# Relu-squared attention into a token mixer on one core: another opening, and key turns of 64 rows in two DMAs

## The chip, the cores and the metric

The kernel runs on one core of a Trainium2 chip. A core has four compute engines, each with an instruction queue of its own that is worked off in order: TensorE (PE; its weight loads are listed as PEld), VectorE (DVE), ScalarE (ACT) and GpSimd (POOL). SyncE (SP) issues DMAs, which 16 DMA engines carry out. TensorE writes to PSUM, from where DVE and ACT copy to SBUF. The metric is the time of one execution on the device in microseconds (us).

## The reference

There are 8 batches of 3200 tokens. With u and v of width 256 and z of width 64, the first half computes

```
scores = (z @ z.T) / S
attn   = max(scores, 0) ** 2
x      = u * (attn @ v)
```

and the second half mixes the tokens of x with three weight matrices:

```
q = x @ w_q ;  k = x @ w_k            # width 64
mixed = (q @ k.T / 8) @ x             # no softmax
out = max(mixed, 0) @ w_out
```

Since nothing nonlinear stands between q, k and x, the kernel computes the small matrix H = k.T @ x (64 x 256) per batch and then q @ H.

## The kernel before, in words

The 3200 rows of a batch are 25 tiles of 128. The columns of the score matrix are cut into seven groups: six of 512 and one of 128 (`widths`). For each group the kernel makes score tiles of 128 x 512, two at a time (a pair, `scores`), in a PSUM tile of two banks; two such tiles ("slots") exist, and all that is not an accumulator goes through them. A pair passes two stages: `first_stage` takes max(x, 0) times 4 on ACT or DVE (tile `g`), `second_stage` squares it on ACT, POOL or rarely DVE (tile `at`, `NAT` buffers). Products of `at` with v accumulate in four other banks (`acc00` to `acc11`, two halves of a group, and two row halves of TensorE, which work at the same time). The attention matrix is symmetric, so part of the `at` tiles are turned by DMA (`tt`) and serve as weights of another group.

When a half of a group is accumulated, ACT or DVE copies one bank, DVE adds the other (`both`), POOL multiplies by u (`x_sb`), and a DMA on SP turns x (`xT_sb`). Then `projections` gives q and k of the group stacked over 128 partitions (`qk`): for r = 0 the queries lie in the upper 64 rows and the keys in the lower, for r = 1 the other way round. `turn_keys` turns the keys by DMA, `heads` multiplies them with x, `heads_out` adds the result to `hacc`, and after a batch's last group the sum `hss` is formed. `mix`, `mix_out`, `proj`, `proj_out` make the output of a batch during the next batch; the last batch's output is made at the end, in a tail written out by hand.

Before the change the turn takes all 128 rows of `qk`, queries too, and `double_keys` on POOL then overwrites the turned queries with a copy of the keys, so that a 128-column weight holds the keys twice and both halves of `hacc` hold the same sums.

The order of all instructions is written by a planner in the kernel: a clock per engine (`clock`), `give(engine, ready, weight)` that books work, `move` and `flush` for DMAs on SP with due times, `at_time` for things at a planned time, `add_extra` for projections, mixes and output products. Constants steer it: `BIAS`, `LATE`, `XWAIT`, `UNTIL`, `lead` (how many score pairs are made ahead), `KEEP`. Before `UNTIL` a pair may be split in two halves on two engines. The planner's costs set the order alone; the chip runs that order by semaphores.

The opening is written by hand. z of batch 0 comes in four pieces (`ZCH`: tiles 0-3, 12-17, 18-24, 4-11), is cast and laid out twice (`cast_first`) and turned on TensorE (`turn_first`); v comes in four pieces on POOL's queue (`load_first_v`). Products on the identity (`warm`) fill TensorE until the first turn.

## Time and profile before

| | |
|---|---|
| median of three runs | 778.13 us (776.56 to 780.9) |
| the profiled execution | 776.21 us, its span 774.4 us |
| busy in the span | PE 99%, ACT 71%, POOL 78%, DVE 67% |
| TensorE busy from 20 to 740 us | 718.54 of 720.00 us |
| TensorE busy from 740 us to the end | 28.61 us |
| DMA queue of SP | 82.6% of 16 engines' span |

A line of a group or timeline gives the source line, engine, operation and tiles (written <- read), the shapes, the count, the duration, and in brackets the idle time of that engine before it and what ended it.

### The profile page before, as it was taken

To read this page: it belongs to the slowest core of one execution; us is meant where nothing else is said; L and a number is where in the kernel's file an instruction comes from. 1 tells how busy PE (TensorE), PEld (TensorE's weight loads), DVE (VectorE), ACT (ScalarE), POOL (GpSimd) and SP (SyncE) were. 2 spreads that over 40 slices of the span, in tenths; PEclk is the share of its full clock that TensorE was granted. 3 is DMA by queue.
4 is the path that set the end of the run, shared out by engine and by line. 5 is a ranking of instruction groups with operands and counts; after the bars stand their busy time and mean duration, and the time that the engine had idled before them with its cause. 6 is when DMAs were issued, how large, how long until landed. Compare 5 with 4: busy or idle time off the path is not lost.

```text
span 774.4 us, 28287 instructions
## 1 busy us (share of the span) xinstructions
PE 762.9 (99%) x12410; PEld 673.8 (87%) x12410; DVE 518.8 (67%) x550; ACT 548.5 (71%) x635; POOL 603.2 (78%) x510
## 2 busy tenths in 40 slices
PE   7999999999999999999999999999999999999996
PEld 6889999889898888988889888998889988898884
DVE  6687687766676566766667657675676756765545
ACT  6686777577666677776877767787587777677734
POOL 7789688888787679867879878778866778878941
PEclk9999999999999999999999999999999999999999
DMA  7999999999999979999999988999999998889745
GB/s 184 157 167 184 133 191 164 169 196 200 187 219 186 198 200 189 174 188 185 207 186 185 201 199 149 198 171 174 229 195 189 161 237 168 162 176 206 144 91 190
DMA packets 307115, 141.10 MB, mean 182 GB/s; under 512 B 285744, under 2 KB 288432, under 8 KB 306992
## 3 DMA queue, kind: packets, MB, share of 16 engines
q1 hardware_dynamic: 300224, 123.13, 82.6%
q0 software_dynamic: 6624, 15.98, 14.8%
q8 instruction: 97, 1.59, 0.9%
q10 hardware_dynamic: 144, 0.20, 0.1%
q14 instruction: 26, 0.21, 0.1%
HBM read 59.64 MB, written 26.21 MB: 111 GB/s over the span
## 4 chain that ended last, share of the span: by engine, by line
PE 94%; DVE 2%; DMA 2%; POOL 1%; issue 0%; ACT 0%; POOLq 0%; DVEq 0%; SPq 0%
PE acc L353 69%; PE sc L265 13%; PE fo L520 6%; PE qk L419 3%; PE qk L457 2%; PE mx L485 1%; DMA v_sb<-in_v_dram 1%; DVE g L291 1%; POOL x_sb L390 1%; DMA z<-in_z_dram 0%; DVE fo L542 0%; DMA xT_sb<-x_sb 0%; DVE both L371 0%; POOL at L310 0%; DVE both L370 0%
## 5 line engine op out<-in xcount | busy, mean ns | idle before, releaser
L353 PE MATMUL acc<-v_sb,at 64*128 64x256 f16 x7344 | 500.8, 269 | 1.3 <-POOL at L310 0.8
L310 POOL TENSOR_TENSOR at<-g 128x1024 f16<-128x1024 f32 (+2 forms) x232 | 414.4, 1799 | 84.8 <-DVE g L291 46.3
L353 PEld LDWEIGHTS <-at 64*128 64x128 f16 x7344 | 403.1, 94 | 52.8 <-issue 7.2
L291 DVE TENSOR_SCALAR g<-sc 128x1024 f32<-128x1024 f32 (+1 forms) x294 | 341.2, 1181 | 107.5 <-PE sc L265 97.4
L307 ACT ACTIVATE at<-g 128x1024 f16<-128x1024 f32 (+1 forms) x250 | 251.3, 1021 | 27.3 <-DVE g L291 24.1
L287 ACT ACTIVATE g<-sc 128x1024 f32<-128x1024 f32 (+2 forms) x184 | 180.5, 984 | 76.6 <-PE sc L265 72.0
L265 PE MATMUL sc<-zT 64*128 64x512 f16 x924 | 186.5, 375 | 2.4 <-DVE g L291 1.4
L390 POOL TENSOR_TENSOR x_sb<-both,u_sb 128x512 f16<-128x512 f32 (+1 forms) x112 | 135.6, 1215 | 63.7 <-DVE both L371 62.9
L353 PE MATMUL acc<-v_sb,tt 64*128 64x256 f16 x2272 | 162.7, 269 | 0.0
L353 PEld LDWEIGHTS <-tt 64*128 64x128 f16 x2272 | 126.6, 94 | 11.1
L371 DVE TENSOR_TENSOR both<-acc,both 128x512 f32<-128x512 f32 (+1 forms) x104 | 69.7, 671 | 23.6 <-ACT both L370 18.7
L265 PEld LDWEIGHTS <-zT 64*128 64x128 f16 x924 | 61.9, 94 | 7.9 <-issue 4.0
L370 ACT COPY both<-acc 128x512 f32<-128x512 f32 (+1 forms) x63 | 36.0, 571 | 45.7 <-PE acc L353 41.8
L542 DVE TENSOR_SCALAR fo<-fo 128x1024 f32<-128x1024 f32 (+2 forms) x30 | 33.1, 1116 | 42.7 <-PE fo L520 42.6
L508 ACT ACTIVATE rt<-mx 128x1024 f16<-128x1024 f32 (+1 forms) x46 | 42.5, 926 | 12.8 <-PE mx L485 12.7
L520 PE MATMUL fo<-wo,rt 128*128 128x256 f16 x400 | 49.5, 274 | 0.1
L370 DVE COPY both<-acc 128x512 f32<-128x512 f32 (+1 forms) x41 | 27.3, 665 | 31.3 <-PE acc L353 28.5
L520 PEld LDWEIGHTS <-rt 128*128 128x128 f16 x400 | 36.4, 98 | 10.7 <-issue 6.5
L433 ACT CAST qk<-qk 128x512 f16<-128x512 f32 (+1 forms) x45 | 24.4, 542 | 25.3 <-PE qk L457 22.7
L547 ACT ACTIVATE fo<-fo 128x1024 f32<-128x1024 f32 (+2 forms) x28 | 24.4, 871 | 23.7 <-PE fo L520 23.0
L472 DVE TENSOR_TENSOR ha<-qk,ha 128x512 f32<-128x512 f32 x37 | 25.5, 688 | 16.7 <-ACT qk L433 16.2
L419 PE MATMUL qk<-xT_sb,wqk 64*128 64x256 f16 (+1 forms) x404 | 32.8, 266 | 0.0
(47 smaller groups left out, 276.4 us busy)
## 6 DMA issues: line engine op xcount, KB each, us to landing
u_sb<-in_u_dram SPq DMA_DIRECT2D x48, 512.0 KB, 4.7
out_dram<-fo SPq DMA_DIRECT2D x46, 512.0 KB, 4.2
v_sb<-in_v_dram POOLq DMA_DIRECT2D x35, 320.0 KB, 6.1
zn<-in_z_dram POOLq DMA_DIRECT2D x7, 400.0 KB, 5.9
tt<-at SPq DMA_TRANSPOSE x143, 4.5
u_sb<-in_u_dram SPq DMA_DIRECT2D x8, 128.0 KB, 3.0
out_dram<-fo SPq DMA_DIRECT2D x8, 128.0 KB, 3.5
out_dram<-fo SPq DMA_DIRECT2D x4, 256.0 KB, 2.6
```

Of the source, the lines that this page charges most:

```text
L265: nc.tensor.matmul(out=sc[:, h, 0:gw], lhsT=z_cols(b, h, ti * P, P), rhs=z_cols(b, h, gs, gw), start=True, stop=True,)
L287: nc.scalar.activation(out=g[:, hs, 0:w], in_=sc[:, hs, 0:w], func=RELU, scale=GSCALE)
L291: nc.vector.tensor_scalar(out=g[:, hs, 0:w], in0=sc[:, hs, 0:w], scalar1=0.0, scalar2=GSCALE, op0=AOP.max, op1=AOP.mult,)
L307: nc.scalar.square(out=out, in_=g[:, hs, 0:w])
L310: mul(out=out, in0=g[:, hs, 0:w], in1=g[:, hs, 0:w])
L353: nc.tensor.matmul(out=accs[half, r][:, ds((j % 2) * D, D)], lhsT=weights(b, gi, ti, j)[top(r), :], rhs=vs[b][top(r), ti, :], start=(first ...
L370: copy(out=both[:, 0 : n * D], in_=accs[half, 0][:, 0 : n * D])
L371: nc.vector.tensor_add(out=both[:, 0 : n * D], in0=accs[half, 1][:, 0 : n * D], in1=both[:, 0 : n * D])
L390: nc.gpsimd.tensor_mul(out=xs[b, gi][:, 0:n, :, r, :].rearrange("p n c d -> p (n c) d"), in0=both[:, 0 : n * D].rearrange("p (m d) -> p m ...
L419: nc.tensor.matmul(out=ps[:, r, 0 : n * P], lhsT=wqk[top(r), c, :, :].rearrange("p t h -> p (t h)"), rhs=xTs[b, gi][top(r), 0:n, c, :], st ...
L508: nc.scalar.activation(out=out, in_=part, func=RELU)
L520: nc.tensor.matmul(out=banks[r][:, ds(j * D, D)], lhsT=flat[:, ds((dc * n + j) * P, P)], rhs=wo[:, dc, :], start=(dc == 0 and j == 0), sto ...
```

## The change

- *Opening.* The warming products read a cleared piece of a weight tile (`blank`) instead of the identity, and are 36; the later five are gone. v's first piece is issued ahead of the identity, its second right after it, its last by the planner at 7.5 us. `first_pair` puts the first pair into two accumulator banks, so that ACT and DVE each take a half. Pairs are no longer split later in the first stage; `UNTIL` is 12 and `on_act` takes ACT at a tie.
- *Keys.* `turn_keys` turns only the 64 rows that hold keys, in one DMA for each r, into one of three tiles of five 64-column blocks. `heads` reads blocks n and n+1 as one 128-column weight: the first 64 output rows are the wanted sums, the others are not used. `double_keys` is gone; `heads_out` adds 64 rows; `hss` is made by two POOL adds, one for each row half.
- *Buffers and planning.* 18 `at` buffers for 16, `KEEP` 4 for 6, `lead` 160 for 140, other `BIAS`, `LATE`, `XWAIT`, `V1`.
- *Tail.* The last batch's `hsum` is made by DVE and POOL, a half each.

```diff
-    NAT = 16
+    NAT = 18
     NX = 7
...
     NEARBY = 8
-    KEEP = 6
+    KEEP = 4
...
         ready = clock[PE] + FROM_PE
-        on_act = max(clock[ACT], ready) < max(clock[DVE], ready)
+        on_act = max(clock[ACT], ready) <= max(clock[DVE], ready)
         copy = nc.scalar.copy if on_act else nc.vector.tensor_copy
...
         for _ in range(n):
-            nc.tensor.matmul(out=idle[:, 0:P], lhsT=ident[:], rhs=ident[:], start=True, stop=True)
+            nc.tensor.matmul(out=idle[:, 0:P], lhsT=blank, rhs=blank, start=True, stop=True)
         clock[PE] += 0.053 * cold() * n
...
-    def scores(p):
+    def scores(p, banks=None):
         assert len(ztimes) >= 4 * tiles[2 * p + 1][0] and p_chunk(p) in z_at, (p, clock, len(ztimes), z_at)
-        sc = ps_tile("sc")
+        sc = banks or ps_tile("sc")
         for h, (b, gi, ti) in enumerate(tiles[2 * p : 2 * p + 2]):
...
             nc.tensor.matmul(
-                out=sc[:, h, 0:gw],
+                out=sc[h][:, 0:gw] if banks else sc[:, h, 0:gw],
                 lhsT=z_cols(b, h, ti * P, P),
...
         for (hs, w), on_act in zip(parts, ways * 2):
+            part = sc[hs.start][:, 0:w] if isinstance(sc, list) else sc[:, hs, 0:w]
             if on_act:
                 nc.scalar.activation(
-                    out=g[:, hs, 0:w], in_=sc[:, hs, 0:w], func=RELU, scale=GSCALE
+                    out=g[:, hs, 0:w], in_=part, func=RELU, scale=GSCALE
                 )
...
                 nc.vector.tensor_scalar(
-                    out=g[:, hs, 0:w], in0=sc[:, hs, 0:w], scalar1=0.0,
+                    out=g[:, hs, 0:w], in0=part, scalar1=0.0,
                     scalar2=GSCALE, op0=AOP.max, op1=AOP.mult,
...
+    kts = [pk.tile([P, 5, dh], FP16, tag=f"kx{i}", name="kx", bufs=1) for i in range(3)]
+
+    def clear_keys():
+        for kt in kts:
+            nc.gpsimd.memset(kt[:], 0.0)
+        give(POOL, 0.0, 0.3)
+
     def turn_keys(b, gi):
-        nn = widths[gi] // P
-        ks[b, gi] = pk.tile([P, 4, 2, dh], FP16, tag="kx", name="kx")
-        nc.sync.dma_start_transpose(
-            out=ks[b, gi][:, 0:nn, :, :].rearrange("p n a h -> p n (a h)"),
-            in_=qks[b, gi][:].rearrange("p r s -> p (r s)")[:, 0 : nn * P],
-        )
-
-    doubled = set()
-
-    def double_keys(b, gi):
-        doubled.add((b, gi))
-        nn = widths[gi] // P
+        n = min(2, widths[gi] // P)
+        ks[b, gi] = kts[(b * NG + gi) % len(kts)]
         for r in halves(gi):
-            sl = slice(2 * r, min(2 * r + 2, nn))
-            nc.gpsimd.tensor_copy(out=ks[b, gi][:, sl, r, :], in_=ks[b, gi][:, sl, 1 - r, :])
+            nc.sync.dma_start_transpose(
+                out=ks[b, gi][:, 2 * r : 2 * r + n, :],
+                in_=qks[b, gi][top(1 - r), r, 0 : n * P],
+            )
...
         nn = widths[gi] // P
-        assert (b, gi) in doubled
+        assert (b, gi) in keys_at
         for n in range(nn):
...
                     out=ps[:, r, D : 2 * D],
-                    lhsT=ks[b, gi][top(r), n, :, :].rearrange("p a h -> p (a h)"),
+                    lhsT=ks[b, gi][top(r), n : n + 2, :].rearrange("p a h -> p (a h)"),
                     rhs=x_rows(b, gi, n)[top(r), :, :],
...
     def heads_out(b, gi, ps):
-        part = ps[:, 0:2, D : 2 * D]
+        part = ps[0:dh, 0:2, D : 2 * D]
         if gi == 0:
-            hacc[b] = psml.tile([P, 2, D], FP32, tag="ha", name="ha")
+            hacc[b] = psml.tile([dh, 2, D], FP32, tag="ha", name="ha", bufs=1)
             nc.vector.tensor_copy(out=hacc[b][:], in_=part)
...
         if gi == LASTG:
-            heads_done(b)
-
-    def heads_done(b):
-        hss[b] = psml.tile([P, D], FP16, tag="hs", name="hs")
-        ha = hacc.pop(b)
-        nc.gpsimd.tensor_add(out=hss[b][:], in0=ha[:, 0, :], in1=ha[:, 1, :])
+            hss[b] = psml.tile([P, D], FP16, tag="hs", name="hs")
+            ha = hacc.pop(b)
+            for r in range(2):
+                nc.gpsimd.tensor_add(out=hss[b][top(r), :], in0=ha[:, 0, :], in1=ha[:, 1, :])
...
+    C3 = 7.0
+    T3 = 10.0
+    V3 = 7.5
     moves = []
...
     def cold():
-        return 2.0 if clock[PE] < 8.4 else 1.0
+        return 2.0 if clock[PE] < 4.6 else 1.0
...
     SPLIT = 0.2
-    UNTIL = 24.0
+    UNTIL = 12.0
...
         return a + BIAS < d
+
+    def first_pair():
+        produced[0] += 1
+        sc = scores(0, [acc_tile(0, r, "sc")[:] for r in range(2)])
+        clock[PE] += 0.22
+        ready = clock[PE] + FROM_PE
+        a, d = give(ACT, ready, 0.6), give(DVE, ready, 0.69)
+        free_at[0] = max(a, d)
+        g = first_stage(0, sc, [True, False])
+        for x, t in zip(tiles, (give(ACT, a, 0.63), give(POOL, d, 1.05))):
+            row_at[x] = t + 0.3
+        for (b, gi, gj, _, nn, _, _), turn in second_stage(0, g, [True, False]):
+            raise AssertionError((b, gi, gj))
...
         a, d = (max(clock[x], ready) for x in (ACT, DVE))
-        if clock[PE] < UNTIL and max(a + 0.57, d + 0.68) + SPLIT < min(a + 1.03, d + 1.2):
-            ways = [a < d, a >= d]
-            done = max(give(ACT, ready, 0.57), give(DVE, ready, 0.68))
-        else:
-            ways = [choose(a, d)]
-            done = give(ACT, ready, 1.03) if ways[0] else give(DVE, ready, 1.2)
+        ways = [choose(a, d)]
+        done = give(ACT, ready, 1.03) if ways[0] else give(DVE, ready, 1.22)
         g = first_stage(p, sc, ways)
...
             ways = [2 if by_dve else by_act]
-            if clock[PE] < UNTIL and max(a + 0.57, c + 0.97) + SPLIT < min(a + 1.06, c + 1.9):
+            if clock[PE] < UNTIL and max(a + 0.63, c + 1.05) + SPLIT < min(a + 1.06, c + 1.9):
                 ways = [a < c, a >= c]
-                done = max(give(ACT, ready, 0.57), give(POOL, ready, 0.97))
+                done = max(give(ACT, ready, 0.63), give(POOL, ready, 1.05))
             else:
...
                 row_at[b, gj, starts[gi] // P + n] = t + 0.5
-
-    def double(b, gi):
-        keys_at[b, gi] = give(POOL, clock[PE], 0.6) + 0.5
-        double_keys(b, gi)
...
             move(
-                done + SLACK, done + 10.0, 1.28, 0.21 * n, lambda: turn_keys(b, gi),
-                lambda t: at_time(t, lambda: double(b, gi)),
+                done + SLACK, done + 10.0, 1.28 * len(halves(gi)), 0.105 * n, lambda: turn_keys(b, gi),
+                lambda t: keys_at.update({(b, gi): t + 0.3}),
             )
...
             if prior[1] == LASTG:
-                give(POOL, done, 0.6)
+                give(POOL, done, 1.4)
                 heads_known(prior[0])
...
         if prior[1] == LASTG:
-            give(POOL, done, 0.6)
+            give(POOL, done, 1.4)
             heads_known(prior[0])
...
     V0 = 56
-    V1 = 11
+    V1 = 8
...
             t0 = max(t + 6, Z0)
-            if b == 0:
-                nc.gpsimd.memset(zn[:, 0 : NT + 2 : NT + 1, :], 0.0)
             at_time(t0, lambda: (load_z(b + 1), push(3.0)))
...
     MORE = 3.0
-    BIAS = 0.2
+    BIAS = -0.2
     XDUE = 5.0
-    XWAIT = 2.0
-    LATE = 0.3
+    XWAIT = 7.0
+    LATE = 0.5
...
-    make_identity(nc, ident)
+    blank = wo[:, 0, 0:P]
+    nc.vector.memset(blank, 0.0)
+    nc.vector.memset(zn[:, 0 : NT + 2 : NT + 1, :], 0.0)
     load_first_z()
     load_first_v(0, 4)
-    idle = acc_tile(0, 1, "warm")
-    warm(28)
+    make_identity(nc, ident)
+    load_first_v(12, 6)
+    idle = acc_tile(1, 0, "warm")
+    warm(36)
     cast_first(0)
...
     cast_first(2)
-    load_first_v(12, 6)
     load_first_v(18, 7)
-    load_first_v(4, 8)
-    clock[:] = [4.4, 4.75, 4.3, 7.0]
-    for t, n0, nn in ((7.0, 0, 4), (18.0, 4, 8), (10.5, 12, 6), (14.0, 18, 7)):
+    clock[:] = [4.5, 4.95, 4.7, 5.6]
+    for t, n0, nn in ((7.2, 0, 4), (15.0, 4, 8), (8.8, 12, 6), (12.0, 18, 7)):
         v_at.update({(0, n): t for n in range(n0, n0 + nn)})
...
     groups.pop(0)
-    use_pair()
+    first_pair()
     use_pair()
     turn_first(2)
-    warm(5)
-    at_time(8.6, lambda: (cast_first(3), give(DVE, 8.6, 0.86)))
-    at_time(10.0, lambda: turn_first(3))
+    at_time(26.0, clear_keys)
+    at_time(C3, lambda: (cast_first(3), give(DVE, C3, 0.9)))
+    at_time(T3, lambda: turn_first(3))
+    at_time(V3, lambda: (load_first_v(4, 8), give(POOL, clock[PE], 0.6)))
     move(10.0, 14.0, 0.55, 1.6, lambda: load_u(0, 0))
...
     done_acc = 0
-    lead = 140
+    lead = 160
     turn_about = False
...
     ha = hacc.pop(last)
-    nc.vector.tensor_add(out=hsum[:], in0=ha[:, 0, :], in1=ha[:, 1, :])
+    for r, add in enumerate((nc.vector.tensor_add, nc.gpsimd.tensor_add)):
+        add(out=hsum[top(r), :], in0=ha[:, 0, :], in1=ha[:, 1, :])
     psl = acc_tile(0, 1, "hl")
...
     ps = ps_tile("qq")
```

More of the change, by code (lines that the diff above doesn't have):

```diff
@@ L1068 @@
                 or (x[1] == "keys" and len(keyed) < 2)
-                or keyed[0] in doubled
+                or keyed[0] in keys_at
             ]
```

## Prediction

> **What bounds the kernel now.** I read the page's first parts, then the busy time in stretches, then TensorE's waits, then the opening as a timeline.
>
> ```profile
> span 774.4 us, 28287 instructions
> PE 762.9 (99%) x12410; PEld 673.8 (87%) x12410; DVE 518.8 (67%) x550; ACT 548.5 (71%) x635; POOL 603.2 (78%) x510
> PE 94%; DVE 2%; DMA 2%; POOL 1%; issue 0%; ACT 0%; POOLq 0%; DVEq 0%; SPq 0%
> ```
> ```profile
> 0.00:26.00 26.00, 21.45 (x294) 17.36 (x296) 18.26 (x24) 18.17 (x29) 20.44 (x27) 1.00 0.74 164
> 26.00:40.00 14.00, 13.84 (x237) 12.63 (x233) 8.33 (x11) 8.63 (x10) 9.53 (x7) 1.00 1.09 169
> 40.00:60.00 20.00, 19.10 (x308) 16.99 (x305) 16.73 (x16) 16.84 (x20) 16.73 (x17) 1.00 1.00 180
> 60.00:100.00 40.00, 40.00 (x687) 39.08 (x684) 28.37 (x31) 27.70 (x31) 32.31 (x29) 1.00 1.08 163
> 100.00:740.00 640.00, 639.89 (x10518) 565.57 (x10515) 430.96 (x449) 465.67 (x528) 516.76 (x426) 1.00 1.01 186
> 740.00:775.00 35.00, 28.61 (x388) 22.22 (x384) 16.15 (x23) 11.50 (x22) 7.43 (x7) 0.97 0.51 151
> ```
>
> In the second fence the first figure after a stretch's length is TensorE's busy time. From 60 to 740 us it stands still for 0.11 us. The change leaves TensorE's work as it is: the program's order has the same matrix products before and after, except 36 warming products for 33. So a gain can come only from the opening, from the 1.06 us that TensorE stands between 26 and 60 us (0.16 + 0.90), and from the tail; a loss can come from anywhere.
>
> ```profile
> PE sc L265 <- DVE g L291: 0.7, 1, 0.7
> ```
>
> This is the largest of TensorE's waits between 26 and 740 us; it lies at 51 us, where a score pair waits for its PSUM slot.
>
> **The opening.** TensorE's rows:
>
> ```profile
> 1.37 3.17 PE L146 MATMUL warm<-ident 128*128 128x128 f16 x28 [1.37 <-POOL ident masks.py:199]
> 4.50 0.83 PE L132 MATMUL ztp<-ident,zd 128*128 128x128 f16 x10
> ...
> 7.32 0.61 PE L265 MATMUL sc<-zT 64*128 64x512 f16 x4 [0.42 <-DVE g L291]
> ```
> ```profile
> 8.69 0.83 PE L353 MATMUL acc<-v_sb,at 64*128 64x256 f16 x12 [0.76 <-POOL at L310]
> 9.34 0.39 PE L265 MATMUL sc<-zT 64*128 64x512 f16 x2
> 9.56 0.29 PE L353 MATMUL acc<-v_sb,at 64*128 64x256 f16 x2
> 10.54 0.62 PE L132 MATMUL ztp<-ident,zd 128*128 128x128 f16 x8 [0.70 <-DVE zd L122]
> ```
> ```profile
> 23.23 2.80 PE L353 MATMUL acc<-v_sb,at 64*128 64x256 f16 x48
> 25.84 0.40 PE L265 MATMUL sc<-zT 64*128 64x512 f16 x2
> ```
> ```profile
> 740.51 5.46 PE acc L353 x100
> ```
> ```profile
> L353 PE MATMUL acc<-v_sb,at 64*128 64x256 f16 x200 | 13.7, 269 | 1.0 <-POOL at L310 0.8 <-DMA v_sb<-in_v_dram 0.3
> L265 PE MATMUL sc<-zT 64*128 64x512 f16 x36 | 6.7, 378 | 1.5 <-DVE g L291 0.6 <-ACT g L287 0.6 <-DVE zT L139 0.2
> ```
>
> A product pair costs 0.109 us (5.46 us for 50), a score pair 0.22 (0.61 for two less 0.39 for one). The first group is 200 products, 10.9 us; it runs from 8.69 to 25.84, in which 13 score pairs (18 by 26 us, less 4 before 8.69 and the one at 25.84), 2.9 us, and eight turns, about 0.45, also run: 14.25 of 17.15 us. So 2.9 us are lost inside the group.
>
> **The change: the opening.** The stages by their rows:
>
> ```profile
> L310 POOL TENSOR_TENSOR at<-g 128x1024 f16<-128x1024 f32 x210 | 394.9, 1892 | 81.6 <-DVE g L291 43.2 <-ACT g L287 25.8 <-DMA tt<-at 5.7
> L291 DVE TENSOR_SCALAR g<-sc 128x1024 f32<-128x1024 f32 x276 | 331.7, 1221 | 101.6 <-PE sc L265 94.0 <-POOL at L310 3.6 <-POOL kx L450 1.9
> L307 ACT ACTIVATE at<-g 128x1024 f16<-128x1024 f32 x232 | 242.0, 1056 | 27.3 <-DVE g L291 24.1
> L287 ACT ACTIVATE g<-sc 128x1024 f32<-128x1024 f32 x170 | 173.5, 1022 | 70.0 <-PE sc L265 69.4
> L370 ACT COPY both<-acc 128x512 f32<-128x512 f32 x59 | 34.5, 584 | 40.6 <-PE acc L353 38.4 <-POOL at L310 0.9 <-POOL x_sb L390 0.7
> ```
> ```profile
> 8.89 1.60 DVE L122 CAST zd<-z 128x512 f16<-128x512 f32 x2
> ```
> ```profile
> v_sb<-in_v_dram POOLq DMA_DIRECT2D x1, 384.0 KB, 7.8
> v_sb<-in_v_dram POOLq DMA_DIRECT2D x1, 256.0 KB, 7.2
> z<-in_z_dram SPq DMA_DIRECT2D x1, 256.0 KB, 6.8
> ```
>
> I follow the new program's queues with these durations. The warming starts about 0.45 us earlier, because it waits for one clear on DVE and no longer for the identity on POOL; its 36 products at 0.107 us (the spacing of the 28) end by about 4.7 us at the latest, where the first turns began at 4.50: nothing gained or lost. Chunk 0's turned block now leaves PSUM on ACT, for which no row stands; DVE took 0.43, ACT's 128x512 copy 0.58; I take the latter: scores from 5.6. Pair 0 is split over two engines without one waiting for the other, until 6.7. DVE does pair 1 until 7.9 (1.22) and so frees the slot for the fourth score pair, until 8.2. v's first piece is issued 0.7 us earlier (it took 7.2 us, landing at 8.6 before), so it lands near 7.9, and the first product runs at about 8.2 instead of 8.69. Next on DVE stands the cast of z's last piece. This landed at 8.5 (6.8 us after issue), so DVE casts from 8.5 to 10.2, takes pair 3 until 11.4, and only then frees the slot for the last turns: TensorE stands from 9.8 to 11.5, longer than the 0.70 it waited there before. At 11.5 eight of the group's 100 product pairs and five of 18 score pairs are done. From there, per two pairs, TensorE needs 2 x (0.22 + 8 x 0.109) = 2.18 us, ACT one g and one square, 2.08, POOL one square, 1.89, DVE one g, 1.22: TensorE is the slowest and need not stand. 92 x 0.109 + 13 x 0.22 + 0.45 = 13.3 us more: the group ends at 24.8 with 18 score pairs done, against 25.84 with 17. That is 1.04 + 0.22, about **1.2 us gained**. Ends: if the cast doesn't wait, DVE is 0.55 us earlier, 1.8 gained; if v's second piece, issued near 2 us instead of 4.87, keeps z's last piece until 11 us, the chain is 2.5 us later and 1.3 is lost. I take the middle, since z's row gives it.
>
> **The middle.** BIAS, LATE, XWAIT, 18 buffers and a lead of 160 change the whole written order. 39 g's go from DVE to ACT (276 to 237, 170 to 216): ACT gains some 37 us with 20 more output scalings and fewer copies, 76% busy at most: no bound. In the order before, the two tightest score pairs near 50 us have 0.54 and 0.76 us of TensorE work until their slot is wanted; after the change none in the middle has under 1.3. So the 0.74 us wait should go: **0.8 us gained**, ends 0 and 1.06.
>
> **The keys.** Removed are 99 doublings on POOL:
>
> ```profile
> L450 POOL COPY kx<-kx 128x128 f16<-128x128 f16 x92 | 24.0, 289 | 2.0 <-DMA kx<-qk 2.0
> L450 POOL COPY kx<-kx 128x64 f16<-128x64 f16 x7 | 1.7, 244 | 0.0
> L479 POOL TENSOR_TENSOR hs<-ha 128x256 f16<-128x256 f32 x7 | 5.1, 724 | 2.3 <-DVE ha L472 2.2
> ```
>
> That is 25.7 us of POOL, less seven more hs adds (5.1) and the three clears: worth nothing while TensorE bounds. Each hs comes 0.7 us later; the first mixes are planned 4 us behind, which hides it (7 x 0.7 = 5 us if not). The products read 128 columns as before. Added are 46 turns (99 for 53), all on SP:
>
> ```profile
> L438 SPq DMA_TRANSPOSE kx<-qk x53: 1177/1226/3407, 49.8 to 743.6; - x53
> L332 SPq DMA_TRANSPOSE tt<-at x143: 1231/1408/5304, 17.9 to 717.3; - x143
> L165 SPq DMA_TRANSPOSE zT<-zn x28: 1215/2023/3059, 41.1 to 627.3; - x28
> ```
>
> A half-size turn has no row; between nothing saved per issue and the longest row it adds 46 x 1.23 = 57 us or 46 x 3.41 = 157 us of SP; I take 57, since the issue's median hardly moves with size (1.23 against tt's 1.41). In the order, from a group's projections to the products that read its keys TensorE has 15.3 us of work at the least, and the path is 0.6 for the cast, 2 x 1.23 and the landing of some 4: hidden, **0**. The Trainium skill, "DMA: Bandwidth & Descriptors" (Rules for kernel authors), speaks against it: two transfers to disjoint partition halves serialize, and one whole transfer is better. By that rule the second of a pair would land a transfer later; no run here shows it yet, and the sum stays, since a second landing of 4 still fits in 15.
>
> **The tail.** hm's second half goes from DVE to POOL and hs waits for both:
>
> ```profile
> 758.45 0.69 DVE L472 TENSOR_TENSOR ha<-hd,ha 128x512 f32<-128x512 f32 x1 [0.23 <-PE hd L457]
> 759.17 0.43 DVE L1111 TENSOR_TENSOR hm<-ha 128x256 f32<-128x256 f32 x1
> 759.70 0.42 DVE L1118 TENSOR_TENSOR hs<-hl,hm 128x256 f16<-128x256 f32 x1
> ```
>
> POOL's add from 759.2 takes 0.72 by the hs row: hs starts near 760.0 instead of 759.70, and mx waits for it: **0.3 us lost** (0 to 0.5). A last output product moves behind the final products, work that TensorE did before them.
>
> **Sum.** -1.2 - 0.8 + 0.3 = -1.7: a span of 772.7, and 776.21 - 1.7 = 774.5 for the profiled run. The runs' median of 778.13 lies 1.9 above that run, so I forecast 776.4 for the median; the three runs spread by 4.3.
>
> **Rivals.** (a) *All idle goes*: 2.9 in the group, 0.5 ahead of it, 1.06 in the middle, no loss in the tail: 4.4, 773.7. For it speaks the rate above, against it the cast behind z. 0.24. (b) *The opening only moves its wait*, z's last piece late behind v: +1.3 - 0.8 + 0.3, 778.9, no measurable change. For it: the DMA engines' share is 0.74 in the opening on average; against it: v's pieces share one queue, so z keeps its own turn. 0.13. (c) *SP falls behind*: per batch seven more issues, 8.6 us, stand ahead of the turns of the next batch's zT; each of seven batch changes that is late by 0.9 us costs 6.3: 782.7. It decides from 0.8 us a change on (5.6 in all). For it: issues of up to 5.3 us show the queue backing up, and POOL waits 5.7 us for tt. Against: TensorE never waits for a turn from 26 to 740 us. 0.13. (d) The five filler products at 6.4 us are dropped and TensorE stands up to 1.7 us; if its rate fell to the 0.107 us spacing for the 3.4 us that it lasts at the start (1.37 to about 4.77), that is 1.7 lost, 778.1. The Trainium skill, "TensorE: Matmul & The Clock Gate" (rules), asks for a gap of about 3 us, so by it this does not happen; the trace, at full spacing after its 0.7 us gaps, agrees as far as it goes. 0.04. The forecast keeps 0.46, alone 774.3 to 778.5.
>
> 0.5% is 3.9 us, about what a measurement can tell from no change. Faster takes (a) and little else: 0.26; slower is (c): 0.13; the rest, 0.61, is within. The range runs from (a) less the runs' spread, 772.8, to short of (c), 781.2.
>
> **What would show it.** First product near 8.2 us; DVE's casts of z's last piece ending near 10.2; the first group ending near 24.8; no wait of TensorE over 0.3 us between 26 and 740; kx turns at about 1.2 us; hs near 0.3 us later in the tail. Wrong if TensorE waits for tt, zT or kx, or if z's last piece lands past 10 us.

## The result, and the profile after

The changed kernel takes 788.28 us in the median (784.57 to 789.66, four runs) against 779.06 for the kernel before on the same chip (776.56 to 780.9): a ratio of 1.0119, 95% interval 1.0091 to 1.0148. It is slower. The forecast was 776.4, with a range up to 781.2. Medians in this text are of all executions of a kernel, ratios leave out those that are over 1.5% above its fastest. The profiled execution took 789.64 us, 13.4 more than the one before.

The head of the page of the changed kernel, and its chain by engine:

```profile
span 787.8 us, 28172 instructions
PE 767.2 (97%) x12413; PEld 673.4 (85%) x12413; DVE 471.2 (60%) x505; ACT 582.5 (74%) x665; POOL 596.7 (76%) x421
PE 92%; DMA 3%; DVE 3%; issue 0%; ACT 0%; POOL 0%; POOLq 0%; DVEq 0%; SPq 0%
```

The same stretches as in the prediction, and the two in which TensorE's clock was halved. Behind the length come the busy times of PE, PEld, DVE, ACT and POOL with their instructions, then the granted clock, the DMA share and GB/s:

```profile
0.00:26.00 26.00, 18.99 (x215) 14.15 (x217) 15.65 (x15) 14.84 (x18) 15.31 (x19) 0.87 0.58 141
26.00:40.00 14.00, 13.83 (x227) 11.98 (x224) 11.68 (x12) 13.26 (x16) 11.84 (x12) 1.00 0.84 130
40.00:60.00 20.00, 20.00 (x334) 18.89 (x331) 12.58 (x14) 17.17 (x19) 18.07 (x14) 1.00 1.11 187
100.00:740.00 640.00, 634.71 (x10405) 556.25 (x10401) 381.25 (x407) 487.80 (x551) 499.15 (x342) 1.00 1.01 179
740.00:788.00 48.00, 39.72 (x570) 33.83 (x568) 24.35 (x32) 19.03 (x31) 16.88 (x13) 0.96 0.45 151
13.18:20.00 6.82, 4.72 (x38) 3.05 (x40) 3.73 (x4) 3.14 (x3) 0.62 (x1) 0.50 0.43 112
713.00:716.30 3.30, 3.01 (x28) 1.98 (x30) 1.23 (x1) 1.54 (x2) 0.37 (x1) 0.50 0.78 289
```

By 26 us TensorE has begun 215 products where it had begun 294. From 100 to 740 it stands for 5.29 us where it stood for 0.11. Only from 40 to 60 us is it better: 20.00 busy for 19.10. Its main waits:

```profile
PE ztp L132 <- DVE g L292: 4.9, 1, 4.9
PE qk L420 <- DMA xT_sb<-x_sb: 2.8, 1, 2.8
PE qk L457 <- DMA kx<-qk: 2.4, 3, 1.1
PE mx L483 <- DVE hs L1126: 0.7, 1, 0.7
PE mx L483 <- DVE ha L472: 0.5, 1, 0.5
```

I use one more measure below, TensorE's *lost time* at a moment: the start of the next product less the work that stands ahead of it, with 0.109 us a product pair, 0.22 a score pair and so on. The work is the same in all kernels here, so lost times compare. Before and after: 9.88 and 14.74 us at 26 us; 11.95 and 15.56 at 65; 15.17 and 22.04 at 700; 15.32 and 26.47 at 720; 17.83 and 30.03 at the last product. So the opening lost 4.9, the stretch to 65 us won 1.2, the main part to 700 lost 3.3, the twenty us behind it 4.3, and the rest 1.0; the way from the last product to the end took 1.2 more. That is 13.4.

*The opening.* The rows of TensorE, DVE and POOL, each from its own timeline of the changed kernel:

```profile
8.55 0.39 PE L265 MATMUL sc<-zT 64*128 64x512 f16 x2 [0.91 <-DVE g L292]
8.77 0.72 PE L354 MATMUL acc<-v_sb,at 64*128 64x256 f16 x10
...
9.89 0.51 PE L354 MATMUL acc<-v_sb,at 64*128 64x256 f16 x6
15.28 1.01 PE L132 MATMUL ztp<-ident,zd 128*128 128x128 f16 x8 [4.88 <-DVE g L292]
```
```profile
8.41 5.68 DVE L122 CAST zd<-z 128x512 f16<-128x512 f32 x2
```
```profile
8.44 0.59 POOL L111 DMA_DIRECT2D v_sb<-in_v_dram  x1
9.05 4.74 POOL L311 TENSOR_TENSOR at<-g 128x512 f16<-128x512 f32 x3
```

The casts of z's last piece took 1.60 us before and 5.68 here: the first of the two 0.417, the second 5.343, from 8.75 to 14.09. POOL's issue of v and three squares behind it without a gap fill just that time (8.44 to 13.80; the row gives the shape of the first square, the other two are twice as wide). The turns wait for the second cast and for the g behind it. The clock is halved from 13.18 to 20.00.

*The last batch.* SP's queue, from its timeline, and TensorE's row behind it:

```profile
702.38 2.64 SPq L333 DMA_TRANSPOSE tt<-at  x2
705.11 2.66 SPq L333 DMA_TRANSPOSE ttl<-at  x1
707.87 0.53 SPq L176 DMA_DIRECT2D u_sb<-in_u_dram  x1
708.45 1.24 SPq L403 DMA_TRANSPOSE xT_sb<-x_sb  x1
```
```profile
713.29 1.03 PE L420 MATMUL qk<-xT_sb,wqk 64*128 64x256 f16 x8 [2.79 <-DMA xT_sb<-x_sb]
```

From 686 to 735 us no gap between two of SP's issues is over 0.10 us; x's turn gets its place at 708.45, lands 4.8 us later, and TensorE has run dry at 710.50. After these 2.79 us stands a window at half clock, the second of the two above.

### The profile page after: what moved, and what is told of

It is laid out like the page before. It is cut to its first block, busy times and chain, and to the rows that moved or that the text cites. A ratio compares the mean times of both kernels' runs of the same rounds, so it can differ in the third digit from the quotient of the medians.

```text
span 787.8 us, 28172 instructions
## 1 busy us (share of the span) xinstructions
PE 767.2 (97%) x12413; PEld 673.4 (85%) x12413; DVE 471.2 (60%) x505; ACT 582.5 (74%) x665; POOL 596.7 (76%) x421
## 2 busy tenths in 40 slices
DMA packets 296364, 137.99 MB, mean 175 GB/s; under 512 B 274992, under 2 KB 277680, under 8 KB 296240
## 4 chain that ended last, share of the span: by engine, by line
PE 92%; DMA 3%; DVE 3%; issue 0%; ACT 0%; POOL 0%; POOLq 0%; DVEq 0%; SPq 0%
PE acc L354 66%; PE sc L265 13%; PE fo L518 6%; DMA kx<-qk 3%; PE qk L420 3%; PE qk L457 2%; PE mx L483 1%; DVE g L292 1%; DVE zd L122 1%; DMA xT_sb<-x_sb 1%; PE warm L146 1%; DVE fo L540 0%; PE ztp L132 0%; DVE ha L472 0%; PE xtx L560 0%
## 5 line engine op out<-in xcount | busy, mean ns | idle before, releaser
L311 POOL TENSOR_TENSOR at<-g 128x1024 f16<-128x1024 f32 (+1 forms) x232 | 425.3, 1848 | 102.0 <-DVE g L292 82.1
L292 DVE TENSOR_SCALAR g<-sc 128x1024 f32<-128x1024 f32 (+2 forms) x248 | 292.6, 1190 | 178.9 <-PE sc L265 176.6
L288 ACT ACTIVATE g<-sc 128x1024 f32<-128x1024 f32 (+2 forms) x223 | 222.7, 1005 | 84.2 <-PE sc L265 81.4
L308 ACT ACTIVATE at<-g 128x1024 f16<-128x1024 f32 (+1 forms) x240 | 243.1, 1032 | 10.5 <-DVE g L292 7.8
L354 PE MATMUL acc<-v_sb,tt 64*128 64x256 f16 x2272 | 156.2, 270 | 0.0
L371 DVE COPY both<-acc 128x512 f32<-128x512 f32 (+1 forms) x51 | 34.9, 685 | 47.1 <-PE acc L354 42.4
L545 ACT ACTIVATE fo<-fo 128x1024 f32<-128x1024 f32 (+2 forms) x49 | 43.1, 921 | 21.0 <-PE fo L518 21.0
L472 DVE TENSOR_TENSOR ha<-qk,ha 64x512 f32<-64x512 f32 x37 | 25.2, 680 | 29.4 <-ACT qk L434 29.4
L506 ACT ACTIVATE rt<-mx 128x1024 f16<-128x1024 f32 (+1 forms) x36 | 32.4, 899 | 10.7 <-PE mx L483 10.4
L457 PE MATMUL qk<-x_sb,kx 64*128 64x256 f16 x360 | 30.2, 269 | 2.5 <-DMA kx<-qk 2.4
```

What stands on the lines that cost most here:

```text
L288: nc.scalar.activation(out=g[:, hs, 0:w], in_=part, func=RELU, scale=GSCALE)
L292: nc.vector.tensor_scalar(out=g[:, hs, 0:w], in0=part, scalar1=0.0, scalar2=GSCALE, op0=AOP.max, op1=AOP.mult,)
L308: nc.scalar.square(out=out, in_=g[:, hs, 0:w])
L311: mul(out=out, in0=g[:, hs, 0:w], in1=g[:, hs, 0:w])
L354: nc.tensor.matmul(out=accs[half, r][:, ds((j % 2) * D, D)], lhsT=weights(b, gi, ti, j)[top(r), :], rhs=vs[b][top(r), ti, :], start=(first ...
L371: copy(out=both[:, 0 : n * D], in_=accs[half, 0][:, 0 : n * D])
```

## Experiments on the opening

The run of each experiment is given as a ratio to the kernel before on its chip, with the 95% interval.

**The second cast on ACT.** Every other queue keeps its order.

```diff
-            (nc.vector.tensor_copy, nc.vector.tensor_copy),
+            (nc.vector.tensor_copy, nc.scalar.copy),
```

> The changed kernel with one instruction moved: the second cast of z's last piece (5.343 us on DVE) goes to ACT's queue; the order on every other engine stays as it is. Theory A (the cast is held by POOL, which ran a DMA issue and three squares back to back beside it): the cast takes 0.4 to 0.7 us, the 4.9 us wait of ztp goes, TensorE's clock is not halved between 13 and 20 us, first group's end is 5 to 8 us earlier, total 780 to 784 us. Rival B (POOL's squares themselves are the bound of the opening and the cast only stands in front of the same wait): TensorE stands as long for squares or for z's columns, total 787 to 790 us.

Measured: 788.42 us, 1.0144 (1.0101 to 1.0186). In the trace of the opening theory A holds: the cast takes 0.62 us, ztp does not wait, the clock stays full there, and the lost time at 26 us is 9.05, below the 9.88 of the kernel before. The time is not the 780 to 784 us of theory A all the same: the profiled run lost 9.8 us between 100 and 140 us, with a stand of 5.8 us for kx and 10.24 us at half clock from 119.2 us on:

```profile
9.60 0.62 ACT L122 CAST zd<-z 128x512 f16<-128x512 f32 x1
```
```profile
PE qk L457 <- DMA kx<-qk: 7.8, 4, 5.8
```

So the cast explains the opening and not the whole.

**POOL's issue moved away from the cast.** The cast is on DVE again.

```diff
+    load_first_v(4, 8)
...
-    at_time(V3, lambda: (load_first_v(4, 8), give(POOL, clock[PE], 0.6)))
+    at_time(V3, lambda: give(POOL, clock[PE], 0.6))
```

> The changed kernel with POOL's issue of v's last piece (8.440 to 9.033 us, in which the second cast of z's last piece began) moved up behind the third piece's, to about 5.4 us; all else in the same order, the cast on DVE again. Theory A, in the form that an instruction on POOL or DVE holds the way to SBUF until it ends and POOL's next one takes it again: POOL is idle at 8.75 us, so the cast takes 0.4 us, TensorE's wait of 4.9 us goes, its lost time at 26 us is 9 to 10 us and not 14.7. If the cast is slow beside any of POOL's squares, it takes 1 us or more and ztp waits. In sum 783 to 787 us or 787 to 790 us.

Measured: 788.2 us (779.06 to 794.99, ten runs), 1.0086 (1.0044 to 1.0128). The casts' row:

```profile
8.31 1.59 DVE L122 CAST zd<-z 128x512 f16<-128x512 f32 x2
```

The second cast took 1.262, not the 0.4 that theory A gave it: POOL's square had begun at 8.474, before it, and the cast finished 0.28 us after that square's end. TensorE still waited 0.8 us for the turns; the lost time at 26 us is 8.93. So the cast is held until an instruction on POOL has ended, and in the changed kernel until a whole run of them has (13.80, with the cast's end at 14.09). The Trainium skill, "SBUF — State Buffer" (SBUF: two separate sides), says that VectorE and GpSimd share a pair of ports under an exclusive lock, held "for the whole instruction". The trace agrees with the lock (0.42 us free, 1.26 behind one square, 5.34 behind an issue and three squares); that POOL kept it over three instructions is more than the rule says, and why it kept it there and gave it up after one here is open.

**The opening alone, as written, and with the cast on ACT.** All else as in the kernel before.

> The kernel before with the opening of the change as it was written, the second cast of z's last piece on DVE: keys, buffers and planning constants as before. Against the same with the cast on ACT (776.22 us) theory A expects the cast at 5.3 us, TensorE 4.5 to 5.5 us behind at 26 us, and with the half clock of one or two windows 780.5 to 783.5 us. Rival B: 776 to 778 us.

Measured: 782.59 us, 1.0066 (1.0046 to 1.0086), lost time at 26 us 13.37. Theory A's numbers.

> The kernel before with the opening alone (warm-up on a zeroed tile, order of the first loads, first pair in the sum banks, no filler products) and z's last cast on ACT; keys, buffers and planning constants of the main part as before. Theory A, now with the cast's 5 us out of the way: the opening keeps the 0.8 us that TensorE gained by 26 us with the cast moved, and the main part is as before, 775.5 to 777.5 us. Rival: the opening's gain is given back in the first batch (v's pieces or weights land late), 777 to 779 us.

Measured: 776.22 us, 0.9982 (0.9964 to 1.0000), lost time 9.28 at 26 us and 15.20 at 700 (before: 15.17). The one cast is worth 6.4 us. Without it the opening is a gain of about 1 us, too small to be told from none.

**No cast on DVE.** Even a single cast is a race: in two of the profiled runs below z's piece landed a little later, and POOL was first; the cast took 4.973 and 2.223 us. DVE and POOL in the first of them (the one named plan_lead_keep):

```profile
9.14 4.97 DVE L122 CAST zd<-z 128x512 f16<-128x512 f32 x1 [0.61 <-DMA z<-in_z_dram]
```
```profile
8.47 0.59 POOL L111 DMA_DIRECT2D v_sb<-in_v_dram  x1
9.08 4.74 POOL L311 TENSOR_TENSOR at<-g 128x512 f16<-128x512 f32 x3
```

```diff
-            (nc.vector.tensor_copy, nc.vector.tensor_copy),
+            (nc.scalar.copy, nc.scalar.copy),
...
-    at_time(C3, lambda: (cast_first(3), give(DVE, C3, 0.9)))
+    at_time(C3, lambda: (cast_first(3), give(ACT, C3, 1.1)))
```

> The opening alone with both casts of z's last piece on ACT, so that none of the two runs on DVE beside POOL's squares (with one on DVE, the cast still took 4.973 and 2.223 us in two of the five profiles, where z's piece came later than POOL's start). Planned so: ACT has 1.2 us more, DVE 0.8 less. Theory A: no cast over 0.7 us, no wait over 1.2 us for ztp, and since the runs no longer depend on that race, 775 to 777 us, faster than before by 0.1 to 0.4%. Rival: ACT's first stages are late by the casts and the gain is lost, 777 to 779 us.

Measured: 780.38 us, 1.0038 (1.0023 to 1.0052), slower. The opening did what was expected (lost time 8.81 at 26 us), but the changed booking gave another order to the whole main part, and by 700 us the kernel was 2.8 us behind the one before (17.94 for 15.17). Neither theory had that.

## Experiments on the keys

**Undone, and done alone.** First the changed kernel with the keys as before (and so 16 buffers):

> The changed kernel with the keys' part undone: one 128-row turn a group, doubled on POOL, 128-row head sums, 16 square buffers; opening, planning constants and cast stay changed. Theory C (the second key transfer on SP's queue makes xT and kx late in the main part: 3.3 us between 65 and 700 us, 4.3 us with the wait of 2.8 us for xT and the half clock behind it at 710 us): those go, the opening's 4.9 us stay, total 781 to 784 us. Rival D (the planning constants, lead and buffers, cause the late stands): they stay or come elsewhere, total 786 to 790 us.

Measured: 785.5 us, 1.0099 (1.0073 to 1.0124). The waits for kx and xT of over 0.3 us are gone but for one of 0.6 for the doubling; the opening's 4.9 us are there; some 8.9 us are lost between 26 and 700 us all the same. Between the two theories.

> The kernel before with the keys' part alone: two 64-row turns a group into three fixed tiles with a zeroed fifth block, 128 columns read, no doubling, head sums on 64 rows, sum of the last batch's heads in halves on DVE and POOL; opening, buffers and planning constants as before. Theory C: 4 to 7 us more than before, with waits for xT or kx in the trace, 782 to 785 us. Rival D: 778 to 780 us, no such wait. The prediction's step put this part at 0 to +0.5 us.

Measured: 788.63 us (783.82 to 789.48), 1.0127 (1.0088 to 1.0166): alone, the keys' part costs about 10 us, more than theory C said. In the profiled execution, the fastest of the four, TensorE waited 2.0 us for xT and 0.9 for kx.

**With the order kept.** In keys_alone the planner knows of the second turn and writes another order. Here it is told the old durations, so that every engine keeps the order of before (lines against keys_alone):

```diff
-                done + SLACK, done + 10.0, 1.28 * len(halves(gi)), 0.105 * n, lambda: turn_keys(b, gi),
-                lambda t: keys_at.update({(b, gi): t + 0.3}),
+                done + SLACK, done + 10.0, 1.28, 0.21 * n, lambda: turn_keys(b, gi),
+                lambda t: at_time(t, lambda: double(b, gi)),
```

with `double` only booking POOL's time. Next, the kernel before whole, with a spare turn behind each key turn; then the kernel before whole, with small loads there, 99 and 198 of them:

```diff
+        n = min(2, nn)
+        if len(halves(gi)) == 2:
+            nc.sync.dma_start_transpose(out=spare_kt[:, 0:n, :], in_=qks[b, gi][top(0), 1, 0 : n * P])
```
```diff
+        for r in halves(gi):
+            nc.sync.dma_start(out=pads[r][:], in_=moe_w_k[0:4, :])
```

The 198 loads are two at each of these places.

> The kernel before with the keys' part, but planned with the durations of before (one issue of 1.28 us a group, the doubling's time still set aside): every engine's order is that of before, SP's queue has 46 more turns, POOL's loses the 99 doublings. Theory E (46 more turns in SP's queue make what stands behind them late, whatever the plan): 782 to 790 us, waits for xT, kx or squares' turns in TensorE's rows. Theory G (the plan, told of the second turn, chose another order, and that order is what costs): 775.5 to 779 us.

> The kernel before, computing all it did in the same order on every engine, with one more turn of 64 rows behind each key turn of a full group (46), into a tile that nobody reads; the doubling stays. Theory E: as slow as the keys with the order kept, 782 to 790 us. If that kernel is slow and this is not, it is the heads' wait for a second transfer and not SP's queue: 777 to 780 us here. Theory G: 776 to 779 us.

> The kernel before with the 99 small loads behind the key turns again (37 us of SP's queue in the padded run), but the plan not told of them, so that every engine's order is that of before. Theory E: slower by 4 us or more, 781 to 787 us, as the padded run with its own plan (785.15). Theory G: the padded run's loss was the plan's, here 776.5 to 780 us.

> The kernel before in its own order on every engine, computing all it did, with 198 small loads behind the key turns in place of 99: some 74 us more of SP's queue, so that it issues about as long (685 us) as in the runs with the extra turns (678 to 693 us), and 0.2 MB more data. Theory E (the hours of SP's queue, whatever fills them): 784 to 792 us, as the spare turns (790.24). Theory F2 (a turn costs more than its issue, in what the turns behind it wait for): 778 to 782 us, about twice the 1.5 us of the 99 loads.

The second column adds up the durations of all DMA rows on SP in the profiled run, the third the wait for xT in TensorE's list:

| kernel, order of before | SP issues, us | TensorE for xT, us | median, us | ratio (95%) |
|---|---|---|---|---|
| before | 612 | 0 | | 1 |
| 99 small loads | 640 | 0.8 | 780.17 | 1.0017 (0.9980 to 1.0053) |
| the keys' part | 678 | 3.5 | 786.46 | 1.0102 (1.0061 to 1.0143) |
| 198 small loads | 681 | 7.4 | 794.14 | 1.0178 (1.0102 to 1.0255) |
| 46 spare turns | 685 | 12.0 | 790.24 | 1.0131 (1.0050 to 1.0212) |

Theory E stands in its main point: nothing that TensorE needs comes from the small loads or the spare turns, the order on every engine is that of before, and both make xT late. More DMAs on SP's queue do it, whatever they move. The cost is not linear: 28 us more cost hardly anything, where theory E had 781 to 787 us and theory G came near (776.5 to 780); 66 to 73 us cost 8 to 14 (the ratios times 777). One such place, SP and TensorE with the spare turns, and then the same turn and products in the kernel before:

```profile
395.29 1.23 SPq L446 DMA_TRANSPOSE kspare<-qk  x1
396.61 1.22 SPq L332 DMA_TRANSPOSE ttl<-at  x1
397.92 1.39 SPq L176 DMA_DIRECT2D u_sb<-in_u_dram  x1
399.37 1.23 SPq L402 DMA_TRANSPOSE xT_sb<-x_sb  x1
```
```profile
407.06 0.64 PE L419 MATMUL qk<-xT_sb,wqk 64*128 64x256 f16 x8 [4.89 <-DMA xT_sb<-x_sb]
```
```profile
379.51 1.24 SPq L402 DMA_TRANSPOSE xT_sb<-x_sb  x1
```
```profile
390.73 0.60 PE L419 MATMUL qk<-xT_sb,wqk 64*128 64x256 f16 x8
```

In the kernel before, this turn was issued 11.2 us ahead of its products and landed after 4.7 us. With the spare turns it was issued 2.8 us before TensorE ran dry at 402.17, and it landed after 7.7 us: it was late at its issue and on its way. Elsewhere it was late on its way alone. The stand of 3.15 us in the same run, from 118.64 us, ended with a turn that was issued 11.1 us ahead (11.8 before) and landed after 14.2 us for 7.5; the stand of 2.59 us with the keys' part, from 180.71 us, with one that landed after 9.0 us for 4.8. So a fuller queue costs ahead of the issue and behind it; what holds a transfer between issue and landing, no run shows.

Added up by stretches of 50 us in which they begin, SP's issues fill 36 to 49 us of each stretch from 50 to 700 in the kernel before, 44 to 49 in the changed one. So the kernel before has stretches as full (48.6 us from 100 us on) with no wait of TensorE behind them; that the changed one is late for want of a free stretch in which to catch up fits this, but was not tested by itself. That doubling is gone from POOL and that the DMA engines move fewer packets (296,364 for 307,115) didn't help.

**Small loads with the planner told of them.**

> The kernel before, computing all it did, with 99 small loads added to SP's queue: behind each key turn one (for the group of 128 rows) or two loads of 1 KB that nobody reads. They take SP's queue 0.5 us each, some 50 us in all, where the second key turn of the changed kernel took it 60 to 67 us (kx 74.4 to 135.2 and 141.9 us), and move 0.1 MB. Theory E (SP's queue is full: it issues 612 us of 774 before, about 94% of every 50 us once the keys are turned twice, and what the planner has timed then lands late): 4 to 9 us slower than before, 781 to 786 us, with waits of TensorE for kx or xT. Theory F (it is the 64-row transfers themselves, their time on the DMA engines or their landing): within 1.5 us of before, 776 to 779 us.

Measured: 785.15 us, 1.0108 (1.0071 to 1.0146), 7 us slower as theory E had it, but with almost no wait for xT (0.6); what grew are small waits for DVE's g and sums. With the order kept the same loads cost 1.5 us, so most of this loss came with the other order and not from the loads: a right number for a wrong reason.

**Loads of u and stores from ACT's queue.**

```diff
-        nc.sync.dma_start(out=us[b, gi][:, 0:nn, :], in_=rows(u, b)[:, n0 : n0 + nn, :])
+        nc.scalar.dma_start(out=us[b, gi][:, 0:nn, :], in_=rows(u, b)[:, n0 : n0 + nn, :])
...
-        proj_out(b, gi, ps, [(not on_act, nc.sync, widths[gi] // P)], stores)
+        proj_out(b, gi, ps, [(not on_act, nc.scalar, widths[gi] // P)], stores)
```

> The kernel with the keys' part alone, and its loads of u and all stores but the last group's issued from ACT's queue rather than SP's: 102 issues of 0.4 to 0.6 us leave SP's queue (681 us to some 625 us, about as before), ACT's queue takes some 50 us more. Theory E: TensorE's waits for xT and kx go, 778 to 782 us, less ACT's new work being hidden. Theory F: the waits for kx stay, 785 to 790 us. If ACT's queue becomes the bound instead (582 us of its time is busy in the changed kernel), the wait of scores for ACT's first stage grows and the time stays above 784 us.

Measured: 829.1 us, 1.0553 (1.0511 to 1.0595). The waits for kx are gone, as E said, but that for xT, which E had going too, is 8.7 us, and a load or a store that has to wait now holds up ACT's first stages. So ACT stood from 461.35 to 466.61 us in front of a store, and TensorE from 463.37 to 468.08 for ACT's g. TensorE's two largest waits:

```profile
PE sc L265 <- ACT g L287: 13.4, 7, 4.7
PE qk L419 <- DMA xT_sb<-x_sb: 8.7, 2, 4.6
```

It decides nothing between the theories.

**x's turn due at once in the last batch.**

```diff
-                t + SLACK, t + XDUE, 1.28, 0.21 * n, lambda: turn_x(b, gi),
+                t + SLACK, t + (XDUE if b < last else 0.0), 1.28, 0.21 * n, lambda: turn_x(b, gi),
```

> The changed kernel with one due time altered: in the last batch a turn of x is due at once rather than 5 us later, so that twice it leaves SP's queue ahead of a load of u or a turn of squares. If the wait of 2.8 us for xT at 710 us and the 3.4 us at half clock behind it come from its place in SP's queue, both go and nothing else changes: 783 to 786 us. If SP's queue as a whole is late there, the wait moves to what was put behind (squares' turns): 787 to 790 us.

Measured: 788.87 us, 1.0146 (1.0110 to 1.0183): no gain. Where the wait went is seen in the profiled execution alone, which took 802.86 us (the other four 787.8 to 791.46): in its last batch TensorE stands for 0.99 us at 699.7, for kx, and for 1.83 at 726.8, for xT, and no longer at 710. There the wait moved.

## Experiments on the planning constants

**All of them, and two halves,** each on the opening with the second cast on ACT and the keys as before.

> The changed kernel with the keys as before (16 buffers) and z's last cast on ACT: opening and planning constants changed, nothing else. If the planning constants (lead 160, a wait of 7 us ahead of a projection, the shifted choice between ACT and DVE, v's loads 8 us apart) are worth nothing, it is level with the opening alone, 775 to 778 us. If they cost the 4 to 5 us that the run with the keys as before lost beside the opening, 780 to 782 us.

Measured: 782.44 us, 1.0074 (1.0045 to 1.0103): 6 us behind the opening alone, as the second case said.

```diff
-    KEEP = 6
+    KEEP = 4
...
-    V1 = 11
+    V1 = 8
...
-    lead = 140
+    lead = 160
```

> The opening with the cast on ACT, and of the planning constants only three: the lead of pairs over products 160 for 140, KEEP 4 for 6, v's loads 8 us apart for 11. All planning constants together took 6 us (782.44 against 776.22). If these three do it, 780 to 783 us; if the choice between engines and the wait ahead of projections do, 775.5 to 778 us.

Measured: 786.33 us, 1.0111 (1.0068 to 1.0154). Some 5 us of its profile are the cast shown above; from 26 to 65 us it lost 4.5 against 1.2 with the opening alone, from 65 to 700 us 8.4 against 4.7. Two of its other runs had a granted clock of 1.000 over the whole run, so no window at half clock as a held cast leaves it, and took 783.36 and 785.27 us.

```diff
-    BIAS = 0.2
+    BIAS = -0.2
...
-    XWAIT = 2.0
-    LATE = 0.3
+    XWAIT = 7.0
+    LATE = 0.5
```

> The opening with the cast on ACT, and of the planning constants only the other three: projections 7 us after x has landed for 2, BIAS -0.2 for 0.2, LATE 0.5 for 0.3 in the choice between ACT and DVE. If these do it, 780 to 783 us, with DVE's first stages near 237 rather than 276 and waits at the sums and mixes; if the lead and KEEP do, 775.5 to 778 us.

Measured: 776.66 us, 0.9996 (0.9973 to 1.0018): nothing. So lead, KEEP and the loads' spacing do it; which of the three was not tried, and 160 was here used with 16 buffers, not 18.

**In the changed kernel itself,** with both casts on ACT and these three as before:

> The changed kernel with both casts of z's last piece on ACT and, of the planning constants, lead, KEEP and the spacing of v's loads as before (140, 6, 11); 18 buffers, keys turned twice, wait and choice as changed. If the second key turn decides with SP's queue at 680 us or more, 782 to 789 us, level with the keys alone (788.63) and the cast on ACT (788.42). If lead and KEEP cost their 6 us here too and add to it, 778 to 782 us.

Measured: 787.18 us (779.91 to 794.88), 1.0099 (1.0067 to 1.0130), TensorE waiting 7.9 us for kx. That is level with the keys alone and with the cast on ACT: the second key turn is enough for it, and the three constants add nothing that can be seen.

## Why the prediction was wrong

*The opening* (-1.2, bounds -1.8 and +1.3). The step that failed is "DVE casts from 8.5 to 10.2", with the 1.60 us of the row before as the price of the pair. That row was 0.419 and 1.265: a cast of 0.42, and one of 0.42 that stood behind a POOL square. A mean over both was read as a duration, and the change put other work on POOL beside it. Measured: 5.343 us for the second, a stand of 4.88 instead of the 1.7 forecast, and half the clock for 6.83 us. Where that cast was off DVE, or held by one square only, the rest of the step holds: a gain of 0.6 to 1.1 us at 26 us in six runs (lost time 8.81 to 9.28, 9.88 before; 9.8 to 11.1 in the eight traces with the opening of before). The first product came at 8.77, not 8.2: v was early (landed at 6.17), but the turns ahead took 1.27 us for 0.83, as the clock was full only from 6.35, and the score pair in front of the product waited for DVE.

*The middle* (-0.8, bounds 0 and -1.06) came out nearly right in its size: 1.2 us were won between 26 and 65 us, and the wait at 51 us is gone. Its reason is not shown: the opening alone, with 16 buffers and all constants of before, has no such wait either and won 0.8 us there.

*The keys* (0) failed by more: about 10 us when done alone, 8 with the order kept. Either failure alone puts the time above the range (788.63 and, for the opening as written, 782.59). The issue's price was right (1,222 ns in the median for 1.23 us assumed), and so was the landing:

```profile
L447 SPq DMA_TRANSPOSE kx<-qk x99: 1166/1222/2552, 65.0 to 751.6; - x99
DMA to landing us min/median/max: 2.3/3.7/9.4
```

What was wrong is "hidden", reckoned as one path of 0.6 + 2 x 1.23 + 4 us against 15.3 us of TensorE's work, as if SP's queue were empty. It was in use for 612 of 774 us. 46 more turns are a matter of that whole queue, and what came late with the order kept was xT, which the step doesn't name; with the changed order it was kx too, the prediction's own sign of being wrong. The rule of the Trainium skill that was weighed there ("DMA: Bandwidth & Descriptors", Rules for kernel authors: halves serialize) advised right; but that the second half lands late is not what the runs show, since loads that nobody reads do the same.

*The rivals.* (c), SP falling behind, had the mechanism with 0.13. Its place was wrong (no wait for zT in the changed kernel) and its price of 6.3 us too low. (a) was not seen: the opening alone, the best of the parts, stayed at 0.9982. (b) was wrong: z's last piece landed at 6.4 us, and at 9.3 us at the latest in the traces with this opening. (d) gave the clock a price for stands up to 1.7 us; in no run did one so short halve it.

*The tail* (+0.3, bounds 0 and 0.5) was nearly right: POOL's half took 0.89 us, hs waited 0.62 for it, and mx 0.67 against 0.2 before, +0.5. This is not all that was lost behind 720 us (2.2 us in the profiled run): 0.50 us is a wait of mx for ha at 752.7 us, and for the rest no cause is shown.

```profile
770.88 0.42 DVE L1119 TENSOR_TENSOR hm<-ha 64x256 f32<-64x256 f32 x1
771.91 0.43 DVE L1126 TENSOR_TENSOR hs<-hl,hm 128x256 f16<-128x256 f32 x1 [0.62 <-POOL hm L1119]
```

*What stays open.* The parts don't add: the opening as written costs about 5 us, the keys about 10, the constants some 6 on top of the opening, and together the change costs about 9. Taking the opening's 5 us away from the changed kernel gave no better median (1.0144 and 1.0086, beside 1.0119). It may be that a TensorE which is ahead only meets the late queue sooner; no run shows it.

## What to carry to other kernels

Add up a queue's own issue time over stretches before calling another DMA on it hidden. Here SP's went from 612 us to 678 and more, nine tenths of nearly every stretch, and the stand showed at another transfer than the one added. A row that groups a few instructions of one kind may hide one that was held: look at each before using the mean as a price. Where a written order changes as a whole with every constant, compare a part with the order kept; otherwise a new order's own 3 to 5 us are taken for the part's.

## What the runs showed of the hardware

*A DVE cast from SBUF to SBUF and POOL's squares exclude each other*, 0.42 us free against up to 5.34. In all 15 casts of this size that were held, in the traces here, the cast ended 0.28 to 0.30 us after an instruction on POOL: nine times after one square, six times only after the last square of a run without a gap. In the nine, the square itself had begun under the cast in front, and took 1.15 us for 1.05; in three of the six the cast began after POOL's issue had ended, so squares alone hold it. The multiplication by u on DVE, with two inputs in SBUF, shows the same near the end. In the kernel before, all four of 512 columns began just ahead of POOL's own multiplication and took 693 ns, and POOL's took 1.77 us where its mean is 1.29. In the changed one POOL was already at work in two cases, with squares and with a multiplication, and DVE's took 1.598 and 1.398. First before, then after:

```profile
L379 DVE TENSOR_TENSOR xd<-both,u_sb 128x512 f16<-128x512 f32 x4 | 2.8, 693 | 0.1
```
```profile
L380 DVE TENSOR_TENSOR xd<-both,u_sb 128x512 f16<-128x512 f32 x4 | 4.4, 1095 | 0.1
```

*The clock changes on a grid of its own.* In all traces here the stretches at half clock inside the kernel are 3.41, 6.83 or 10.24 us long, one to three times 3.413, and programs that begin alike are granted the full clock at any time from 3.75 to 6.54 us (warm-up from 0.99 us). No stand of TensorE up to 1.98 us was followed by half clock; of those from 2.07 to 2.82 some were and some not; all from 3.15 us on were. The Trainium skill, "TensorE: Matmul & The Clock Gate" (Part 1), has a free-running window of 3,413 ns, which agrees; its rule of no gaps over about 3 us (Why this matters for your kernels) is a little generous, as stands of 2.07 and 2.59 us here were followed by half clock.
